# Half-wise loads of the first block, sink value rows by GpSimd transfers, joint sink scores and one more crossbar transpose in an attention and channel-mix kernel

## The chip, the cores and the metric

The kernel runs on one core of a Trainium2 chip. The metric is the time of one execution on the device in microseconds. Of the kernel before, three runs were timed; of one execution there is a profile with the start and end of every instruction.

## The reference

Sliding-window attention with four sink positions, and on its result an RWKV channel mix. Batch 4, 8 heads of 64, 768 positions, d_model 512, d_ff 1024.

```python
scores = scale * np.matmul(q, k.transpose(0, 1, 3, 2))
is_sink = pos[None, :] < int(n_sink)             # n_sink = 4
in_window = (rel >= 0) & (rel < int(window))     # window = 128
scores = np.where(is_sink | in_window, scores, -1e9)
a = softmax(scores); attn = np.matmul(a, v)
x = attn.transpose(0, 2, 1, 3).reshape(B, S, H * D)
x_prev = x shifted by one position
xk = mu_k * x + (1 - mu_k) * x_prev
xr = mu_r * x + (1 - mu_r) * x_prev
k = np.maximum(xk @ w_k, 0.0)
out = sigmoid(xr @ w_r) * ((k * k) @ w_v)
```

## The kernel before

The work is cut into 12 units: each of the 4 batches has three blocks of 256 positions (T is 0, 1, 2). A unit goes through four stages, one function each.

`load` issues the transfers of q, k and v on SP's queue. A unit's q and k come in two transfers each, one for each half of the partitions, and v in two for its two groups of 128 positions. `load_weight` issues the five 1 MB transfers of w_k (two halves, wka and wkb), w_r and w_v.

`prepare` casts q, k and v to bf16 (tiles kb, qb, vb; line L543 or L536), turns q and k so that the head dimension lies on the partitions, and copies them from PSUM to kt and qt (L589). The turning is done by PE transposes (L576), and for the units in KD and QD by the crossbar, a transposing transfer on SP's queue (L562). For T = 0 it also prepares the sinks. ksink holds the four sink keys of all heads (GpSimd, L670). vsink holds the four sink value rows of each head, each in the rows of that head: a matmul with the constant matrix spread copies the first four rows of vb to the partitions where they belong (L676), and VectorE multiplies them by hmask, which keeps one head in each row (L680).

`attend` computes a unit's scores (L721), exponentials on ScalarE (L775), masks on VectorE (L789) and products with v (L808), then 1/sum (L822) and x (L825). In blocks 1 and 2 of a batch the sinks lie outside the window, so scores with ksink (L696), their exponentials es (L703) and products with vsink (L763) are added. In block 0 the sinks lie inside the window or before it, and no such group is needed.

`mix` turns x into xt, by PE transposes (L849) and copies from PSUM (L858), or by the crossbar (L869) for the units in XD, which are 9, 10 and 11. It then forms the difference td (L877), xk and xr (L888). `ffn` has the products with w_k (L939), the relu (L949 on ScalarE, L953 on VectorE), its square kk (L967, L963), the products with w_r (L979) with the sigmoid (L985), and those with w_v (L997), whose result is multiplied (L1006) and stored (L1013). The last unit's last products are in `last_product` (L909, L919, L924).

The order of everything is fixed by three tables of numbers that were worked out outside the kernel. The functions only register operations in the list P.op; ORDER gives the order in which they are emitted (a negative number is a fill matmul on the tile warm, L1018, that computes nothing), CHOICE says which engine takes an operation that several could take, and SLOTS says which buffer each tile takes. Each engine runs its own instructions in that order and waits for the others by semaphores.

PSUM has two tiles of two banks for scores (sc) and four single banks (bank) for everything else, so a product's bank must be evacuated before another can be written to it. Loads of q, k and v have three buffers each, weights in fp32 three.

`fill`, `fill_later` and the `make_` functions set constants at the start. VectorE sets ones, spread, hmask, ksink, vsink and others, GpSimd makes ident, masks, spread and hmask. The casts of the weights follow the loads: w_k in four quarters, of which a unit's first products need the first.

Of the kernel before, what the change touches and what calls it, by code (L numbers as in the profile page):

```python
# [8 lines left out]
FP32 = mybir.dt.float32  # L9
# [9 lines left out]
    92: "ACT", 93: "ACT", 94: "ACT", 95: "ACT", 97: "ACT", 100: "ACT", 102: "DVE", 105: "DVE",  # L19
    110: "DVE", 111: "DVE", 114: "ACT", 115: "DVE", 139: "POOL", 142: "POOL", 145: "POOL", 148:  # L20
    "DVE", 150: "DVE", 151: "ACT", 152: "ACT", 154: "DVE", 161: "DVE", 191: "DVE", 193: "DVE",
    194: "DVE", 197: "DVE", 199: "DVE", 200: "DVE", 203: "DVE", 204: "DVE", 213: "DVE", 230:
    "ACT", 234: "ACT", 273: "DVE", 276: "DVE", 279: "DVE", 282: "DVE", 285: "ACT", 286: "ACT",
    298: "DVE", 306: "DVE", 315: "ACT", 354: "DVE", 364: "ACT", 365: "DVE", 367: "DVE", 383:
    "ACT", 387: "ACT", 436: "DVE", 439: "DVE", 444: "DVE", 445: "DVE", 467: "ACT", 475: "ACT",
    514: "DVE", 516: "DVE", 521: "DVE", 524: "ACT", 525: "ACT", 546: "ACT", 550: "ACT", 554:
    "ACT", 558: "ACT", 595: "DVE", 598: "DVE", 603: "ACT", 604: "ACT", 606: "DVE", 634: "ACT",
    681: "DVE", 682: "DVE", 691: "DVE", 700: "ACT", 704: "ACT", 708: "ACT", 755: "DVE", 759:
    "DVE", 760: "ACT", 772: "DVE", 781: "ACT", 785: "ACT", 789: "ACT", 834: "DVE", 836: "DVE",
    837: "DVE", 853: "ACT", 856: "DVE", 857: "ACT", 860: "DVE", 861: "ACT", 904: "DVE", 906:  # L30
    "DVE", 910: "DVE", 912: "DVE", 913: "DVE", 929: "ACT", 933: "ACT", 940: "DVE", 941: "ACT",
    994: "DVE", 995: "ACT", 999: "ACT", 1003: "ACT", 1007: "ACT", 1022: "DVE", 1026: "DVE",
    1034: "DVE", 1035: "ACT",
# [5 lines left out]
XD = (9,10,11)  # L39
# [7 lines left out]
JOINT = ()  # L47
# [5 lines left out]
BY_ACT = ()  # L53

# [131 lines left out]
def kernel(  # L186
# [14 lines left out]
    nc = tc.nc  # L201
# [198 lines left out]
    def fill():  # L400
        for t, value in ((ones, 1.0), (spread, 0.0), (hmask, 1.0)):
            nc.vector.memset(t, value)
        if VS:
            nc.vector.memset(pick, 0.0)
# [670 lines left out]
```

## Time and profile before

| what | value |
|---|---|
| median of 3 runs | 165.98 us (165.54 to 166.24) |
| span of the profiled execution, first to last instruction | 164.3 us |
| mean granted clock of TensorE | 0.999 |
| bytes moved | 34.60 MB, mean 211 GB/s |

The span is that of one execution under the profiler; the time of a run is taken around the whole execution and holds a little more than from the first to the last instruction, here 1.7 us. In the rows of the profile an engine with q behind its name (SPq) is its queue of issues, PEld is the weight load of PE. A row of a timeline gives the start, the time until its end, the engine, the line, the operation, the tile that is written and those that are read, and in brackets the idle time ahead of it and who ended it.

### The profile page before, as it was taken

The page shows a single profiled execution, that of the slowest core. Times are in us where ns is not written, and L with a number is a line of the kernel's source. Part 1 is how long each engine was busy: PE and PEld are TensorE (multiplying, and loading weights), DVE is VectorE, ACT ScalarE, POOL GpSimd, SP SyncE. Part 2 cuts the span into 40 slices and gives each one's busy share as a digit, 9 for nine tenths or more (in the row PEclk, how much of TensorE's full clock was granted, in tenths as well). Part 3 has the DMA queues.
Part 4 walks back from the last instruction along what each step waited for, and adds up shares of the span by engine and source line. Part 5 has one row for each costly group of instructions (what it writes and reads, how often), then busy time and mean ns, then how long its engine had stood idle before and what let it go on. Part 6 is the DMA issues. An engine that isn't in the chain of part 4 may idle for free.

```text
span 164.3 us, 4195 instructions
## 1 busy us (share of the span) xinstructions
PE 158.4 (96%) x1603; PEld 102.6 (62%) x1603; DVE 145.4 (89%) x381; ACT 131.2 (80%) x218; POOL 13.5 (8%) x38
## 2 busy tenths in 40 slices
PE   6999889999999999999999999999999999999992
PEld 2455568866467587577566775856575765664851
DVE  5259999999999999989999999999999999789752
ACT  3277999999999999999999999997668759163240
POOL 6409300010000000060000000000000000000000
PEclk9999999999999999999999999999999999999999
DMA  4999999999969896999999887986996955077743
GB/s 120 247 305 311 348 335 355 301 354 210 228 154 270 135 240 148 234 198 167 224 216 157 188 156 163 235 146 150 199 123 136 362 149 200 0 90 297 262 185 128
DMA packets 79042, 34.60 MB, mean 211 GB/s; under 512 B 67112, under 2 KB 73520, under 8 KB 79024
## 3 DMA queue, kind: packets, MB, share of 16 engines
q1 hardware_dynamic: 79008, 34.35, 86.3%
q8 instruction: 12, 0.20, 0.6%
q14 instruction: 6, 0.05, 0.1%
q10 hardware_dynamic: 16, 0.00, 0.0%
HBM read 24.12 MB, written 6.29 MB: 185 GB/s over the span
## 4 chain that ended last, share of the span: by engine, by line
PE 79%; ACT 8%; SPq 4%; DMA 3%; issue 2%; DVE 1%; POOL 1%; DVEq 0%; ACTq 0%; POOLq 0%
PE bank L997 23%; PE bank L939 23%; PE bank L979 12%; PE bank L808 6%; PE sc L721 6%; SPq L337 3%; DMA qs<-in_q_dram 3%; PE bank L576 2%; ACT e L775 2%; PE bank L849 2%; ACT rl L949 1%; PE bank L763 1%; ACT qt L589 1%; PE bank L909 1%; PE bank L1018 1%
## 5 line engine op out<-in xcount | busy, mean ns | idle before, releaser
L775 ACT ACTIVATE e<-sc 128x1024 bf16<-128x1024 f32 (+1 forms) x48 | 46.1, 994 | 1.8 <-PE sc L721 1.7
L939 PE MATMUL bank<-xk,wk_sb 128*128 128x256 bf16 x384 | 47.1, 273 | 0.0
L997 PE MATMUL bank<-wv_h,kk 128*128 128x512 bf16 x184 | 43.1, 379 | 0.1
L939 PEld LDWEIGHTS <-wk_sb 128*128 128x128 bf16 x384 | 36.4, 98 | 7.4 <-issue 0.4
L949 ACT ACTIVATE rl<-bank 128x512 bf16<-128x512 f32 x40 | 24.2, 625 | 8.6 <-PE bank L939 7.1
L997 PEld LDWEIGHTS <-kk 128*128 128x128 bf16 x184 | 17.1, 98 | 17.8 <-issue 0.4
L789 DVE TENSOR_TENSOR e<-e,mask 128x1024 bf16<-128x1024 bf16 (+1 forms) x40 | 25.4, 642 | 0.7 <-ACT e L775 0.5
L979 PE MATMUL bank<-wr_sb,xr 128*128 128x512 bf16 x96 | 23.7, 379 | 0.0
L888 DVE SCALAR_TENSOR_TENSOR xk<-td,mu_all,xt 128x256 bf16<-128x256 bf16 x48 | 22.4, 483 | 0.3
L888 DVE SCALAR_TENSOR_TENSOR xr<-td,mu_all,xt 128x256 bf16<-128x256 bf16 x48 | 22.1, 475 | 0.2
L967 ACT ACTIVATE kk<-rl 128x512 bf16<-128x512 bf16 x29 | 18.3, 664 | 4.2 <-DVE rl L953 4.0
L985 ACT ACTIVATE th<-bank 128x512 f32<-128x512 f32 x24 | 15.1, 646 | 5.7 <-PE bank L979 5.7
L825 DVE TENSOR_TENSOR x<-bank,rec 128x256 bf16<-128x256 f32 x48 | 19.2, 416 | 0.4
L808 PE MATMUL bank<-vb,e 128*128 128x65 bf16 x352 | 16.6, 194 | 0.0
L1006 DVE SCALAR_TENSOR_TENSOR w<-th,bank 128x512 f32<-128x512 f32 x19 | 13.0, 682 | 3.6 <-issue 1.8
L808 PEld LDWEIGHTS <-e 128*128 128x128 bf16 x352 | 13.6, 97 | 3.5
L979 PEld LDWEIGHTS <-xr 128*128 128x128 bf16 x96 | 8.8, 98 | 8.6 <-issue 0.2
L721 PE MATMUL sc<-qt,kt 64*128 64x128 bf16 (+1 forms) x256 | 13.9, 238 | 0.0
L721 PEld LDWEIGHTS <-kt 64*128 64x128 bf16 x256 | 8.9, 94 | 5.7 <-issue 3.1
L1018 PE MATMUL bank<-warm 128*128 128x512 bf16 x30 | 10.6, 484 | 1.1 <-DVE warm L1038 1.1
L877 DVE TENSOR_TENSOR td<-xt 128x512 bf16<-128x512 bf16 x24 | 10.3, 428 | 0.7 <-ACT xt L858 0.5
L589 ACT COPY qt<-bank 128x512 bf16<-128x512 bf16 x15 | 9.4, 643 | 1.0 <-PE bank L576 1.0
(74 smaller groups left out, 161.7 us busy)
## 6 DMA issues: line engine op xcount, KB each, us to landing
ks<-in_k_dram SPq DMA_DIRECT2D x24, 256.0 KB, 4.7
qs<-in_q_dram SPq DMA_DIRECT2D x24, 256.0 KB, 4.4
vs<-in_v_dram SPq DMA_DIRECT2D x24, 256.0 KB, 4.4
out_dram<-w SPq DMA_DIRECT2D x19, 256.0 KB, 2.7
w<-in_moe_w_k_dram SPq DMA_DIRECT2D x2, 1024.0 KB, 10.4
w<-in_moe_w_v_dram SPq DMA_DIRECT2D x2, 1024.0 KB, 9.3
w<-in_moe_w_r_dram SPq DMA_DIRECT2D x1, 1024.0 KB, 9.7
out_dram<-ob SPq DMA_DIRECT2D x4, 256.0 KB, 2.6
```

Of the source, the lines that this page charges most:

```text
L721: nc.tensor.matmul(out=sc[:, a, o0:o1], lhsT=lhs[rows], rhs=rhs[rows], start=u not in BIAS, stop=True, skip_group_check=u in BIAS)
L775: nc.scalar.activation(out=buf[ek][:, :, lo:], in_=buf[sck][:, :, lo:], func=AF.Exp, scale=scale)
L789: nc.vector.tensor_tensor(out=at, in0=at, in1=m, op=ALU.mult)
L808: nc.tensor.matmul(out=o[:, g, a, :], lhsT=e[:, a, e0:e0 + 128], rhs=rhs, start=(T == 0 and i == 0), stop=(i == len(blocks) - 1), skip_gro ...
L825: P.op("DVE", dve(256), lambda ok=ok, rk=rk, c=c: nc.vector.tensor_tensor(out=buf["x", u][:, :, 128 * c:128 * c + 128].rearrange("p g (a d ...
L888: nc.vector.scalar_tensor_tensor(out=buf[key][:, c, :], in0=buf[tk][:, i, :], scalar=mu[w][:, c:c + 1], in1=xt[:, c, t0 - 1:t0 + 255], op0 ...
L939: nc.tensor.matmul(out=ps[:, i, :], lhsT=wk_sb[:, c, 128 * f:128 * f + 128], rhs=xk[:, c, :], start=(c == 0), stop=(c == NC - 1), skip_gro ...
L949: nc.scalar.activation(out=buf[rk], in_=buf[psk].rearrange("p (i t) -> p i t", i=2), func=AF.Relu)
L967: nc.scalar.activation(out=buf["kk", u][:, 2 * f2:2 * f2 + 2, :], in_=buf[rk], func=AF.Square)
L979: nc.tensor.matmul(out=buf[psk], lhsT=buf["xr", u][:, c, 128 * g:128 * g + 128], rhs=wr_sb[:, c, :], start=(c == 0), stop=(c == NC - 1))
L985: P.op("ACT", act(512), lambda psk=psk, tk=tk: nc.scalar.activation(out=buf[tk], in_=buf[psk], func=AF.Tanh, scale=0.5), rank + 4 + g, tak ...
L997: nc.tensor.matmul(out=buf[psk], rhs=wv_h[:, f, :], lhsT=buf["kk", u][:, f, 128 * g:128 * g + 128], start=(f == 0), stop=(f == NF - 1))
```

## The change

The change has these parts:

- **Half-wise loads.** For units in BY_HALF (only unit 0) the q and k transfers are cut once more, by heads: eight transfers instead of four, first half of the heads of q, of k, then the second halves. `prepare` already works on halves of the heads.
- **Sink value rows.** A new fp32 tile vstage of 128 x 4 x 64 receives the four sink rows of v of all batches by four transfers of GpSimd, straight to the partitions where they belong. The product with hmask reads it there. The matmul with spread, spread itself and the bank that it needed go. The rows of a head move (from 4a to 16a within 32), so ksink and hmask change with them.
- **Joint sink scores.** JOINT becomes (0, 1, 2, 3): for each batch the scores with ksink and their exponentials are computed for blocks 1 and 2 together, in one bank and one activation of 512 columns.
- **Crossbar for unit 8.** XD becomes (8, 9, 10, 11).
- **Short memsets.** 20 one-column memsets of a tile spare on VectorE at the end of `fill_later`, 24 on GpSimd behind the mask. They compute nothing.
- **Tables.** CHOICE, ORDER and SLOTS are new throughout. ORDER has 26 fill matmuls instead of 30. In all, VectorE has 20 instructions more, which are the short memsets, and else 2 less; ScalarE has 1 less; GpSimd no longer takes the three casts of k and q that it had.

```diff
-XD = (9,10,11)
+XD = (8, 9, 10, 11)
-JOINT = ()
+JOINT = (0, 1, 2, 3)
+BY_HALF = (0,)
...
 ORDER = (
-    80, 81, 78, 82, 87, 83, 84, 77, -1, -2, -3, -4, -1, -2, 90, 0, 1, 79, 102, 108, -2, -3, -4,
+    80, 82, 84, 85, 83, 78, 2, 0, 77, 79, 108, 81, 92, -1, -2, -3, -4, -1, -2, -3, -4, 109, 93,
...
+            if u in BY_HALF:
+                rows = src[b, :, 256 * T:256 * T + 256, :].rearrange(
+                    "(w l) (p j) d -> w p l (j d)", w=2, j=4)
+
+                def by_half(key=key, rows=rows, half=0):
+                    for w in range(2):
+                        nc.sync.dma_start(
+                            out=buf[key][w::2, 4 * half:4 * half + 4, :, :].rearrange(
+                                "p (l x) j d -> p l (x j d)", x=2),
+                            in_=rows[w][:, 2 * half:2 * half + 2])
...
-    spread = tile1([128, 128], BF16, "spread")
+    vstage = tile1([128, B, D], FP32, "vstage")
+    spare = tile1([128, 48], FP32, "spare")
+
+    def short(engine, lo, hi):
+        for i in range(lo, hi):
+            engine.memset(spare[:, i:i + 1], 0.0)
...
-        for t in ksink + vsink:
+        for t in ksink + vsink + [vstage]:
             nc.vector.memset(t, 0.0)
...
+        short(nc.vector, 24, 44)
...
         window_mask(mask.rearrange("p k q -> p (k q)"), ones, 0.0)
+        short(nc.gpsimd, 0, 24)
...
-            keep(m, -4 * a, [[-32, NP], [0, D + 1]], 1, m)
-            keep(m, 3 + 4 * a, [[32, NP], [0, D + 1]], -1, m)
+            keep(m, -16 * a, [[-32, NP], [0, D + 1]], 1, m)
+            keep(m, 3 + 16 * a, [[32, NP], [0, D + 1]], -1, m)
...
+    for i in range(NS):
+        P.op("POOL", 1000.0, lambda i=i: nc.gpsimd.dma_start(
+            out=vstage[i::16], in_=v[:, :, i, :].rearrange("b h d -> h b d")), -50,
+            service=60.0, descs=32, reads=["stage0"], writes=[("vstage", i)])
...
-                nc.gpsimd.tensor_copy(out=kz[rows, :, 4 * a:4 * a + NS],
+                nc.gpsimd.tensor_copy(out=kz[rows, :, 16 * a:16 * a + NS],
...
-        P.op("PE", 220.0, lambda: nc.tensor.matmul(
-            out=buf[psk].rearrange("p (h d) -> p h d", h=H), lhsT=spread,
-            rhs=buf["vb", u][:, 0, :, 0:D], start=True, stop=True), rank + 4, lag=PE_LAG,
...
-            in0=buf[psk].rearrange("p (h d) -> p h d", h=H)), rank + 4, hold=[psk],
+                in0=vstage[:, b, :].unsqueeze(1).to_broadcast([128, H, D]))
```

Three places show how the tables move instructions. The first is the start of SP's queue, on which all loads are issued: first the kernel before, then the changed one (ks, qs and vs are the fp32 tiles of k, q and v; x2 stands for two issues alike).

```order
L337 DMA ks_67<-in_k_dram 64x4x256 x2
L337 DMA qs_70<-in_q_dram 64x4x256 x2
L307 DMA vs_73<-in_v_dram 128x8x64 x2
L337 DMA ks_68<-in_k_dram 64x4x256
L337 DMA qs_71<-in_q_dram 64x4x256 x2
```

```order
L353 DMA qs_70<-in_q_dram 64x2x256 x2
L353 DMA ks_67<-in_k_dram 64x2x256 x2
L353 DMA qs_70<-in_q_dram 64x2x256 x2
L353 DMA ks_67<-in_k_dram 64x2x256 x2
L320 DMA vs_73<-in_v_dram 128x8x64 x2
L368 DMA qs_71<-in_q_dram 64x4x256 x2
```

The four whole loads of unit 0 became eight half ones, with q ahead of k, and v of unit 0 stands behind eight issues instead of four.

The second is the same queue where the weights are loaded, before and then changed (w_76 and w_77 are buffers of the weights; ks_67 is unit 3's k here, vs_75 unit 2's v).

```order
L354 DMA w_76<-in_moe_w_k_dram 128x4x512
L354 DMA w_77<-in_moe_w_k_dram 128x4x512
L307 DMA vs_75<-in_v_dram 128x8x64
L337 DMA ks_67<-in_k_dram 64x4x256 x2
L354 DMA w_78<-in_moe_w_r_dram 128x4x512
L307 DMA vs_75<-in_v_dram 128x8x64
L337 DMA qs_70<-in_q_dram 64x4x256 x2
L354 DMA w_76<-in_moe_w_v_dram 128x4x512
```

```order
L385 DMA w_76<-in_moe_w_k_dram 128x4x512
L368 DMA ks_67<-in_k_dram 64x4x256 x2
L320 DMA vs_75<-in_v_dram 128x8x64 x2
L385 DMA w_77<-in_moe_w_k_dram 128x4x512
L368 DMA qs_70<-in_q_dram 64x4x256 x2
L385 DMA w_78<-in_moe_w_r_dram 128x4x512
L385 DMA w_76<-in_moe_w_v_dram 128x4x512
```

Four loads of 256 KB moved ahead of the second half of w_k.

The third is ScalarE's queue up to its cast of the first quarter of w_k (wk_sb), before and then changed (e are the exponentials, es those of the sinks, kt, qt and xt copies from PSUM).

```order
L775 ACTIVATE e_97<-sc_62 128x1024
L775 ACTIVATE e_93<-sc_61 128x1024
L589 COPY kt_86<-bank_63 128x2x256
L703 ACTIVATE es_98<-bank_66 128x256
L589 COPY qt_91<-bank_64 128x2x256
L646 CAST vb_136<-vs_74 128x8x64
L775 ACTIVATE e_94<-sc_61 128x1024
L589 COPY qt_91<-bank_65 128x2x256
L775 ACTIVATE e_95<-sc_62 128x1024
L703 ACTIVATE es_99<-bank_65 128x256
L501 ACTIVATE wk_sb<-w_76 128x4x256
```

```order
L626 COPY kt_86<-bank_65 128x2x256
L683 CAST vb_136<-vs_74 128x8x64
L741 ACTIVATE es_98<-bank_66 128x512
L813 ACTIVATE e_93<-sc_62 128x1024
L813 ACTIVATE e_95<-sc_61 128x1024
L580 CAST kb_81<-ks_69 128x2x4x64
L896 COPY xt_155<-bank_63 128x2x256
L626 COPY kt_87<-bank_64 128x2x256
L626 COPY kt_87<-bank_63 128x2x256
L813 ACTIVATE e_96<-sc_62 128x1024
L538 ACTIVATE wk_sb<-w_76 128x4x256
```

The cast of w_k moved behind unit 2's k (kt_87) and a fifth wide exponential; the two es of 256 columns became one of 512. From the first exponential to this cast ScalarE had 18 instructions and now has 23. At the other end of the program, unit 11's x, which ends the chain of dependent work, goes to the crossbar behind unit 11's last value products; between those and the first product that needs it PE had 32 key products and 40 products of 512 columns, and now has 16 and 40.

More of the change, by code (lines that the diff above doesn't have):

```diff
@@ L18 @@
 CHOICE = {
[L19 to L30, printed above, removed]
@@ L446, in make_bias1 @@
         window_mask(early.bitcast(BF16)[:, 384:640], warm[:, 0:128], LOW)
-    def make_spread():
-        for a in range(2):
-            nc.gpsimd.tensor_copy(
-                out=spread[0:NS, :].rearrange("p (c w) -> p c w", w=32)[:, :, 4 * a:4 * a + NS],
-                in_=ident[0:NS, 0:NS].unsqueeze(1).to_broadcast([NS, NP, NS]))
     def make_hmask():
```

57 lines of the change are left out of this document (46 added, 11 removed), and 154 rows, old and new, of tables (ORDER, SLOTS).

## The prediction

> **What bounds the kernel now.** I read the page first: busy shares, slices, chain.
>
> ```profile
> PE 158.4 (96%) x1603; PEld 102.6 (62%) x1603; DVE 145.4 (89%) x381; ACT 131.2 (80%) x218; POOL 13.5 (8%) x38
> ...
> PE   6999889999999999999999999999999999999992
> ...
> ACT  3277999999999999999999999997668759163240
> ...
> PEclk9999999999999999999999999999999999999999
> ...
> PE 79%; ACT 8%; SPq 4%; DMA 3%; issue 2%; DVE 1%; POOL 1%; DVEq 0%; ACTq 0%; POOLq 0%
> ```
>
> PE is busy nearly always and carries 79% of the chain, at a clock that was never cut. But ACT's row is at 9 as well for two thirds of the span, so I ask next where PE is the limit and where it waits. The table by stretches gives, after each stretch and its length, the busy time of PE, PEld, DVE, ACT and POOL, the clock, the DMA share and GB/s.
>
> ```profile
> 12.00:18.00 6.00, 5.29 (x68) 3.17 (x66) 5.71 (x17) 4.67 (x8) 5.23 (x13) 1.00 1.10 304
> 18.00:24.00 6.00, 5.44 (x85) 3.55 (x85) 5.93 (x19) 6.00 (x11) 0.00 (x0) 1.00 1.08 360
> 24.00:44.00 20.00, 20.00 (x212) 14.00 (x212) 19.79 (x52) 20.00 (x33) 0.74 (x2) 1.00 1.03 299
> ...
> 104.00:124.00 20.00, 20.00 (x207) 13.18 (x205) 19.65 (x54) 16.16 (x28) 0.00 (x0) 1.00 0.99 166
> ```
>
> From 24 us on PE has no gap to speak of. Before that it has gaps, and DVE and ACT set the pace (5.93 and 6.00 of 6.00 in 18 to 24). So there are two questions: when does the gapless part start, and how much PE work is left from there. The timeline of PE (start, us, engine, line, what) shows the start, the first products with wk (L939), and what matmuls cost when they follow each other.
>
> ```profile
> 16.77 0.38 PE L676 MATMUL bank<-vb,spread 128*128 128x512 bf16 x1
> 16.99 0.39 PE L576 MATMUL bank<-ident,kb 128*128 128x128 bf16 x4
> ...
> 23.54 0.59 PE L1018 MATMUL bank<-warm 128*128 128x512 bf16 x2
> 23.98 1.05 PE L939 MATMUL bank<-xk,wk_sb 128*128 128x256 bf16 x8
> 24.87 0.39 PE L849 MATMUL bank<-ident,x 128*128 128x128 bf16 x4
> 25.09 0.39 PE L576 MATMUL bank<-ident,kb 128*128 128x128 bf16 x4
> ...
> 128.80 0.93 PE L939 MATMUL bank<-xk,wk_sb 128*128 128x256 bf16 x7
> 129.66 0.29 PE L696 MATMUL bank<-qt,ksink 128*32 128x256 bf16 x4
> 129.88 0.61 PE L721 MATMUL sc<-qt,kt 64*128 64x256 bf16 x12
> ```
>
> A matmul costs the distance to the next start, not its own 0.2 to 0.4 us: 0.22 for 512 columns (16.77 to 16.99, and two in 23.54 to 23.98), 0.111 for 256 (eight in 0.89), 0.055 for 128 (four in 0.22). A group of four sink scores takes 0.22, and entering it 0.08 more (seven products of 0.111 are 0.78, the distance is 0.86).
>
> **The change, part by part: PE after the start.** Removed behind the first wk product are three of the four spread products (the first lies ahead of it): 3 x 0.22 = 0.66. Unit 8's x goes by crossbar, which drops eight transposes: 8 x 0.055 = 0.44. Joint sink scores turn two groups of four into one of eight; four of them run side by side, so the second four add 0.11 where a group of its own costs 0.22 + 0.08: 0.19 less for each batch, 0.57 for the three behind the start. Sum: **1.67 us less**. The fill matmuls (30 to 26), and the same savings of batch 0, lie ahead of the start in time that PE waits through, and are worth nothing.
>
> **The start.** It is set by ACT, whose queue must get through the exponentials of units 0 and 1 before its cast of the first wk quarter (L501). Rows of ACT and of the first DVE cast:
>
> ```profile
> 7.61 0.43 DVE L543 CAST qb<-qs 128x512 bf16<-128x512 f32 x1 [2.31 <-DMA qs<-in_q_dram]
> ...
> 9.91 1.51 ACT L775 ACTIVATE e<-sc 128x768 bf16<-128x768 f32 x2
> ...
> 12.80 1.51 ACT L775 ACTIVATE e<-sc 128x768 bf16<-128x768 f32 x2 [0.55 <-PE sc L721]
> 14.20 0.59 ACT L589 COPY qt<-bank 128x512 bf16<-128x512 bf16 x1
> ...
> 16.68 1.94 ACT L775 ACTIVATE e<-sc 128x1024 bf16<-128x1024 f32 x2 [0.31 <-PE sc L721]
> 18.51 0.59 ACT L589 COPY kt<-bank 128x512 bf16<-128x512 bf16 x1
> 18.98 0.41 ACT L703 ACTIVATE es<-bank 128x256 bf16<-128x256 f32 x1
> 19.25 0.62 ACT L589 COPY qt<-bank 128x512 bf16<-128x512 bf16 x1
> 19.72 0.66 ACT L646 CAST vb<-vs 128x512 bf16<-128x512 f32 x1
> 20.29 1.02 ACT L775 ACTIVATE e<-sc 128x1024 bf16<-128x1024 f32 x1
> ...
> 22.85 1.08 ACT L501 ACTIVATE wk_sb<-w 128x1024 bf16<-128x1024 f32 x1
> ```
>
> Distances from start to start: 0.70 for a narrow exponential (12.80 to 14.20, two), 0.915 for a wide one (16.68 to 18.51), 0.47 for a copy, 0.57 for a cast, 0.27 for es. Before, ACT has 18 instructions from the first exponential to the wk cast: 4 narrow, 4 wide, 6 copies, 2 casts, 2 es, together 10.96, in 12.94 us; so some 2 us are waits. The new order puts 23 there: 4 narrow, 5 wide, 9 copies, 4 casts and one es of 512 (I take a copy's 0.47): 2.80 + 4.58 + 4.23 + 2.28 + 0.47 = **14.4 us**, 3.4 more. Three casts that GpSimd did are part of it.
>
> Against that stands an earlier first exponential. The landing of q ends the wait at 7.61, and 2.3 us later (cast, transpose, copy, scores) comes the exponential at 9.91. The DMA issues and the landing medians:
>
> ```profile
> 0.81 1.41 SPq L337 DMA_DIRECT2D ks<-in_k_dram  x2
> 2.27 1.27 SPq L337 DMA_DIRECT2D qs<-in_q_dram  x2
> ...
> out_dram<-w SPq DMA_DIRECT2D x19, 256.0 KB, 2.7
> ...
> w<-in_moe_w_k_dram SPq DMA_DIRECT2D x2, 1024.0 KB, 10.4
> ...
> out_dram<-w SPq DMA_DIRECT2D x2, 128.0 KB, 1.7
> ```
>
> Four issues took 2.9 us however large the transfers are, so the four first halves are issued by about 3.5, the last at about 2.9. Before, the last of four whole ones was issued there too, and landed 4.7 us later. A half-size store landed 1.0 us sooner than a whole one (1.7 against 2.7), and half the bytes lie ahead: I bound the last first half by 5.1 and 6.6 and take 5.7. The first exponential is then at 8.0 (7.4 to 8.9), some 1.9 us sooner.
>
> The Trainium skill, "DMA: Bandwidth & Descriptors", "Rules for kernel authors", speaks against splitting: two transfers to disjoint partition halves serialize, and one large transfer is better. The rows above agree that a transfer of half the size takes well over half the time (1.7 of 2.7), but they also show it landing sooner; this kernel split by partitions before already. If by that rule nothing at all were gained, it would be the last rival below.
>
> Waits of ACT in the new stretch: 1.5 us (0.5 if all that it does is fed, 3 if unit 1's k, which lands about as late as before, holds it). From the start of the wk cast to the first product 1.1 (22.85 to 23.98). Start: 8.0 + 14.4 + 1.5 + 1.1 = **25.0**, against 23.98: 1.0 later. DVE must also do some 40 instructions from unit 0's v to its own wk cast, and v stands behind four more issues; this ends no earlier, so I give the start no less than 23.4.
>
> **Parts that I cost at nothing.** The memsets on spare run on DVE while it waits for q and k, and on GpSimd, which has nothing to do from 18 to 24 us (0.00 of 6.00). GpSimd's four loads of sink rows: no such transfer is in the trace; vsink is first needed at about 17 us and they are issued by about 9, so even the 10.4 of the largest transfer would cost 2 us at most, the 2.7 of a store nothing; I take 0. Unit 8's two crossbar transposes add two issues to SP's queue, ahead of later keys' transposes: 0 to 1.0 us, I take 0. At the end, unit 11's x:
>
> ```profile
> 142.79 3.65 SPq L869 DMA_TRANSPOSE xt<-x  x2
> ...
> xt<-x SPq DMA_TRANSPOSE x6, 3.5
> ...
> 152.41 3.49 PE bank L939 x32
> ```
>
> Before, PE has other work for 9.6 us between these transposes and the first product that needs them. Behind unit 11's last value products stood 32 key products and 40 of 512 columns, 32 x 0.111 + 40 x 0.22 = 12.4; now 16 and 40 stand there, 10.6, and the 9.6 shrink to 7.8. If landing (3.5, the second issued 1.2 later) and DVE's differences and mixing take the whole of 9 us, PE waits 1.2. I count 0: nothing shows that the 9.6 were used up.
>
> **Sum.** Span 164.3 + 1.0 - 1.67 = 163.6. The median of the runs, 165.98, lies 1.7 above the profiled span. **165.3 us**.
>
> **Rivals.** (a) *The earlier scores are carried through.* With the exponential at 7.4 and waits of 0.5 the start is at 23.4: 164.3 - 0.6 - 1.67 = 162.0, so 163.7; if also the gapless part loses less than now, down to 162.6. For it: nothing but DMA holds the first scores. Against: DVE's 5.93 of 6.00.
>
> (b) *Weights late, slower.* The second half of wk was issued as the second of these two and landed 10.4 later:
>
> ```profile
> L354 SPq DMA_DIRECT2D w<-in_moe_w_k_dram x2: 676/1310/1943, 13.6 to 14.3; - x2
> ```
>
> That is 24.7. Now unit 3's k and unit 2's v, four loads of 256 KB, stand ahead of it. At 360 and 299 GB/s their 1.05 MB take 2.9 and 3.5 us, the additional issues up to 2.4: it lands at 27.6 to 30.6. Its cast on DVE or ACT takes 1.1, behind perhaps one exponential of 0.9: ready at 28.7 to 32.6. PE needs it after 32 key products (3.55), 12 transposes (0.66) and two half groups of scores with their value products (about 1.2): 25.0 + 5.4 = 30.4. At the late end PE waits 2.2 us: 167.5. It is slower by the bound below once the cast ends after 31.9. In all three later weights the same lateness is then already paid. For it: PE has no reserve behind 24 us, ACT is at 20.00 of 20.00. Against: the middle of the range, 30.6, costs next to nothing.
>
> (c) *The halves do not land sooner.* First exponential at 9.9 as before, start at 26.9: 164.3 + 2.9 - 1.67 = 165.5, so 167.2. Against it stand the two stores.
>
> **How the numbers follow.** A difference of 0.5% (0.83 us: 165.15 and 166.81) is about what a measurement of this kernel can tell from no change. Forecast 0.42, rival (a) 0.27, (b) 0.22, (c) 0.09. The forecast lies just inside the bound, and its own spread (164.5 to 166.6) is cut by it: 0.16 of its 0.42 count as faster. Of (b) and (c) 0.06 stay within the bound. Faster 0.43, same 0.32, slower 0.25. The range leaves out about one in ten at each end: 162.7 to 167.5.
>
> **What would show it.** Right: the first exponential near 8.0; the first wk product at 25 with a gapless PE behind it; a PE whose remaining work is 1.7 us shorter; sink score groups of eight with 0.33 to the next. Wrong: a wait of PE on the wk, wr or wv casts after 29 us (b); a first exponential after 9 (c); a start before 24 (a); a wait of PE for xk in the last 20 us, or of DVE for the sink rows at 17. If the stalls that PE has within 24 to 160 us shrink or grow, which I hold equal, the sum is wrong at that place.

## The result, and the profile after

| what | before | after |
|---|---|---|
| median of 5 runs | 166.07 us (165.54 to 166.40) | 168.12 us (167.12 to 168.60) |
| span of the profiled execution | 164.3 us | 166.9 us |
| ratio after to before | | 1.0105 [1.0072, 1.0138] |

The change makes the kernel about 1% slower. The profiled execution took 168.60 us and is the longest of the five; the spans of the others are 165.4 to 166.4 us, and the time around the span is 1.7 us in all of them. So what the rows below lose is more than a usual execution loses; the unaltered kernel was profiled once more as e18, with a span of 165.3 us. The page of the changed kernel, with the same rows as before: busy shares, slices of PE, ACT and the clock, and the chain that ended last by engine.

```profile
PE 158.9 (95%) x1587; PEld 101.8 (61%) x1587; DVE 143.7 (86%) x399; ACT 132.2 (79%) x217; POOL 12.0 (7%) x61
...
PE   7998979999999899999899999999999999999991
...
ACT  3467999999999998997999999969678949532350
PEclk9999999999999999999999999999999999999999
...
PE 14%; DMA 3%; DVE 2%; issue 0%; SPq 0%; DVEq 0%
```

PE's row now has two slices at 8 in the stretch that was all 9 before. The chain was 79% PE before, and now it can be followed back only to a transfer. In order of time it begins (start, us, what):

```profile
133.69 4.05 DMA xt<-x
...
137.83 0.77 DVE td L915 x2
138.59 0.79 DVE xk L926 x2
...
140.83 0.27 PE bank L977
```

A crossbar transpose (unit 10's x), the differences that wait for it, xk, and the product that waits for xk: a transfer, not PE, was last here. PE was idle for only 0.13 us ahead of that product, so this row shows the kind of the wait and not what was lost. The table by stretches (PE, PEld, DVE, ACT, POOL, clock, DMA share, GB/s) tells how much PE lost, where before had 19.89 us or more in each of these stretches:

```profile
44.00:64.00 20.00, 19.20 (x210) 12.45 (x208) 18.32 (x48) 18.60 (x33) 0.00 (x0) 1.00 1.08 222
64.00:84.00 20.00, 19.56 (x207) 12.75 (x204) 19.15 (x54) 18.66 (x33) 0.60 (x2) 1.00 1.13 208
...
104.00:124.00 20.00, 19.68 (x194) 11.71 (x192) 19.23 (x51) 16.33 (x28) 0.00 (x0) 1.00 1.07 157
```

The three have 1.56 us without PE work, at a full clock. The start shows in ScalarE's timeline, as in the prediction:

```profile
9.01 1.51 ACT L813 ACTIVATE e<-sc 128x768 bf16<-128x768 f32 x2 [1.45 <-PE sc L759]
...
11.66 1.51 ACT L813 ACTIVATE e<-sc 128x768 bf16<-128x768 f32 x2 [0.60 <-PE sc L759]
...
14.78 0.62 ACT L580 CAST kb<-ks 128x512 bf16<-128x512 f32 x1 [1.11 <-DMA ks<-in_k_dram]
...
17.19 1.94 ACT L813 ACTIVATE e<-sc 128x1024 bf16<-128x1024 f32 x2 [0.22 <-PE sc L759]
...
22.77 0.67 ACT L580 CAST kb<-ks 128x512 bf16<-128x512 f32 x1
23.46 0.58 ACT L896 COPY xt<-bank 128x512 bf16<-128x512 bf16 x1
23.94 1.16 ACT L626 COPY kt<-bank 128x512 bf16<-128x512 bf16 x2
25.09 1.02 ACT L813 ACTIVATE e<-sc 128x1024 bf16<-128x1024 f32 x1
26.01 1.05 ACT L538 ACTIVATE wk_sb<-w 128x1024 bf16<-128x1024 f32 x1
```

and VectorE's cast of w_k:

```profile
25.66 0.69 DVE L544 CAST wk_sb<-w 128x1024 bf16<-128x1024 f32 x1
```

The first exponential is 0.9 us sooner than before (9.01 against 9.91), but ScalarE's queue waits for unit 1's k until 14.78, and the first product with w_k comes at 26.41 instead of 23.98, when VectorE's cast has ended. The landing medians of loads and crossbar transposes, after:

```profile
qs<-in_q_dram SPq DMA_DIRECT2D x4, 128.0 KB, 2.6
ks<-in_k_dram SPq DMA_DIRECT2D x4, 128.0 KB, 2.7
kt<-kb SPq DMA_TRANSPOSE x16, 3.8
...
qt<-qb SPq DMA_TRANSPOSE x8, 4.1
...
vstage<-in_v_dram POOLq DMA_DIRECT2D x4, 8.0 KB, 2.9
```

and before:

```profile
kt<-kb SPq DMA_TRANSPOSE x16, 3.6
...
qt<-qb SPq DMA_TRANSPOSE x8, 2.4
```

Four key times carry the comparison from here on (first exponential, first product with w_k, start of the last matmul, span):

| | exponential | w_k product | last matmul | span |
|---|---|---|---|---|
| before | 9.91 | 23.98 | 160.83 | 164.25 |
| after | 9.01 | 26.41 | 163.28 | 166.90 |

From the first w_k product to the last matmul it is 136.85 us before and 136.87 after. So 2.43 us were lost at the start, none were won behind it, and 0.2 us went in the last stores.

### The profile page after: what moved, and what is told of

Read it like the earlier page. It is cut to its first block, busy times and chain, and to the rows that moved or that the text cites. A ratio compares the mean times of both kernels' runs of the same rounds, so it can differ in the third digit from the quotient of the medians.

```text
span 166.9 us, 4218 instructions
## 1 busy us (share of the span) xinstructions
PE 158.9 (95%) x1587; PEld 101.8 (61%) x1587; DVE 143.7 (86%) x399; ACT 132.2 (79%) x217; POOL 12.0 (7%) x61
## 5 line engine op out<-in xcount | busy, mean ns | idle before, releaser
L813 ACT ACTIVATE e<-sc 128x1024 bf16<-128x1024 f32 (+1 forms) x48 | 45.0, 959 | 4.3 <-PE sc L759 4.3
L977 PE MATMUL bank<-xk,wk_sb 128*128 128x256 bf16 x384 | 48.0, 273 | 0.3
L1035 PE MATMUL bank<-wv_h,kk 128*128 128x512 bf16 x184 | 44.0, 379 | 0.1
L987 ACT ACTIVATE rl<-bank 128x512 bf16<-128x512 f32 x44 | 25.7, 606 | 7.4 <-PE bank L977 6.3
L827 DVE TENSOR_TENSOR e<-e,mask 128x1024 bf16<-128x1024 bf16 (+1 forms) x40 | 25.2, 644 | 0.1
L926 DVE SCALAR_TENSOR_TENSOR xk<-td,mu_all,xt 128x256 bf16<-128x256 bf16 x48 | 21.7, 479 | 0.1
L1023 ACT ACTIVATE th<-bank 128x512 f32<-128x512 f32 x24 | 14.2, 601 | 8.7 <-PE bank L1017 8.5
L1005 ACT ACTIVATE kk<-rl 128x512 bf16<-128x512 bf16 x24 | 14.8, 632 | 2.8 <-DVE rl L991 2.7
L1044 DVE SCALAR_TENSOR_TENSOR w<-th,bank 128x512 f32<-128x512 f32 x18 | 12.1, 684 | 2.0 <-PE bank L1035 1.3
L683 ACT CAST vb<-vs 128x512 bf16<-128x512 f32 x17 | 10.5, 634 | 1.2 <-DMA vs<-in_v_dram 1.2
L1001 DVE TENSOR_TENSOR kk<-rl 128x512 bf16<-128x512 bf16 x24 | 9.8, 415 | 1.8 <-ACT rl L987 1.8
```

Source lines behind the costliest of these rows:

```text
L813: nc.scalar.activation(out=buf[ek][:, :, lo:], in_=buf[sck][:, :, lo:], func=AF.Exp, scale=scale)
L827: nc.vector.tensor_tensor(out=at, in0=at, in1=m, op=ALU.mult)
L926: nc.vector.scalar_tensor_tensor(out=buf[key][:, c, :], in0=buf[tk][:, i, :], scalar=mu[w][:, c:c + 1], in1=xt[:, c, t0 - 1:t0 + 255], op0 ...
L977: nc.tensor.matmul(out=ps[:, i, :], lhsT=wk_sb[:, c, 128 * f:128 * f + 128], rhs=xk[:, c, :], start=(c == 0), stop=(c == NC - 1), skip_gro ...
L987: nc.scalar.activation(out=buf[rk], in_=buf[psk].rearrange("p (i t) -> p i t", i=2), func=AF.Relu)
L1005: nc.scalar.activation(out=buf["kk", u][:, 2 * f2:2 * f2 + 2, :], in_=buf[rk], func=AF.Square)
```

## The experiments

Two questions: what sets the start, and where the saved PE work went. Three theories are named below. **L**: the start is set by the landing of unit 1's k and the queue behind it, not by the first exponential. **H**: behind the start VectorE's queue paces the changed order. **D**: behind the start transfers come late. "Start" is the first product with w_k, "behind" the time from it to the last matmul. All ratios are to the kernel before, run on the same chip. Of each run one execution was profiled; times within a run are from that one.

**What sets the start.** The first four edits are of the changed kernel. In e1 the casts of the first two quarters of w_k come sooner, one on VectorE and one on ScalarE, and four fills go; ScalarE's part of the edit:

```diff
+L538 ACTIVATE wk_sb<-w_76 128x4x256
 L813 ACTIVATE e_96<-sc_62 128x1024
-L538 ACTIVATE wk_sb<-w_76 128x4x256
```

> The changed kernel with the casts of the first two quarters of w_k moved forward (VectorE's ahead of the difference td of unit 1, ScalarE's ahead of unit 2's first exponential) and the four fill matmuls ahead of the first w_k product taken out. The weight has landed at 23.8 us. Theory P (PE's own work from the first product sets the end): the first product starts near 25.4 instead of 26.4 and the whole run is about 1.0 us faster than the changed kernel. Theory H (ScalarE and VectorE set the pace in the middle, PE only waits elsewhere): the first product is as early, but the run changes by less than 0.3 us, since the casts only change places with exponentials.

170.28 us, 1.0243 [1.0207, 1.0280]. The first exponential was at 7.82, the start at 26.12, 0.3 us sooner than after instead of the expected 1.0, and "behind" became longer, 139.08 us: the sigmoids (L1023) are 0.2 us later than after's at first, up to 0.4 sooner in between and 1.9 later at the end. Neither expectation held; moving the casts ahead gave nothing.

In e2 four fills are added between 5 and 8 us, where PE has gaps, to see whether its slow first products come from these.

```diff
+four fill matmuls among unit 0's first transposes and scores (ORDER)
```

> The changed kernel with four more fill matmuls between 4.8 and 8 us, where its PE has gaps. If PE's slow pace there (0.32 us for 384 columns where 0.16 is seen later) comes from these gaps, the four bias products take 0.65 instead of 1.3 us, the first exponential starts at about 8.2 instead of 9.0, and by theory P the end comes 0.5 to 0.8 us earlier if ScalarE's queue passes it on. If the slow pace has nothing to do with the gaps, the bias products stay at 0.32 each and the first exponential comes at 9.0 to 9.4.

168.66 us, 1.0158 [1.0119, 1.0196]. The exponential came sooner than in after, 8.16, and the start was at 26.81, not sooner but 0.4 later. An earlier exponential is worth nothing here. That the fills made it earlier is not shown: it was at 8.28 in e18, without them.

e3 loads unit 0 whole, in the changed order.

```diff
-BY_HALF = (0,)
+BY_HALF = ()
```

> The changed kernel with unit 0's q and k loaded whole (four issues of 256 KB, q first), all else as it is. If half loads bring the start forward, the first exponential comes later than 9.0, at about 9.5 to 10, and the first w_k product later than 26.4 by as much; the run is 0.5 to 1.0 us slower than the changed kernel. If the four additional issues cost more than the halves bring, all later loads land some 2 us of issue time earlier (v of unit 0 near 9.7 instead of 10.7), the first product comes at 25 to 26 and the run is faster by 0.5 or more.

170.81 us, 1.0285 [1.0240, 1.0330]; exponential 11.52, start 29.11, both later than expected. In the changed order, with q ahead of k, the half loads are worth 2.7 us at the start.

e7 issues the two first halves of unit 0's k from ScalarE, so that SP has two issues less ahead of unit 1.

```diff
-                        nc.sync.dma_start(
+                        queue = nc.scalar if key[0] == "k" and half == 0 else nc.sync
+                        queue.dma_start(
```

> The changed kernel with the two transfers of the first half of unit 0's k issued by ScalarE's queue instead of SP's, so that all later loads are issued 1.3 us sooner; ScalarE issues them ahead of its table load. Theory L (the start is set by the loads of units 1 and 2, which the four additional issues push back): unit 1's k lands near 13.4 to 13.8 instead of 14.7, the first w_k product comes at 25.2 to 25.8 instead of 26.4, and the run is 0.6 to 1.2 us faster than the changed kernel. Theory A (ScalarE's longer queue from the first exponential on sets it): no change of the first product beyond 0.3 us.

168.67 us (167.56 to 169.19), 1.0171 [1.0138, 1.0203]. ScalarE's timeline of e7:

```profile
7.80 1.51 ACT L814 ACTIVATE e<-sc 128x768 bf16<-128x768 f32 x2 [0.60 <-PE sc L760]
...
14.28 0.62 ACT L581 CAST kb<-ks 128x512 bf16<-128x512 f32 x1 [1.83 <-DMA ks<-in_k_dram]
...
25.51 1.05 ACT L539 ACTIVATE wk_sb<-w 128x1024 bf16<-128x1024 f32 x1
```

and of e6 (below), which leaves the start alone:

```profile
7.68 1.51 ACT L813 ACTIVATE e<-sc 128x768 bf16<-128x768 f32 x2 [0.60 <-PE sc L759]
...
15.12 0.62 ACT L580 CAST kb<-ks 128x512 bf16<-128x512 f32 x1 [1.83 <-DMA ks<-in_k_dram]
...
26.34 1.05 ACT L538 ACTIVATE wk_sb<-w 128x1024 bf16<-128x1024 f32 x1
```

The exponentials differ by 0.12, the casts of unit 1's k by 0.84, and the casts of w_k by 0.83 as well. Over eight executions of the changed order (after, e2, e6, e7, e9, e13, e17, e18) this cast starts at 14.28 to 15.19, the exponential at 7.68 to 9.01, and the distance from the cast to the start is 11.62 us in every one. (In e3 and e15, whose loads come otherwise, it was 12.80 and 12.96.) So L holds; it rests on this distance and not on e7's shift, since the cast was at 14.46 in e18 without the edit. For the total e7 gave nothing: its start is 25.90, 0.5 sooner (25.2 to 25.8 was expected), and its median is no better than after's, so what is lost behind the start varies by more than that.

e8 puts the half loads alone into the old order.

```diff
+BY_HALF = (0,)
```

> The kernel before with the half-wise loads alone (k's first half, q's, then the second halves; the cast of k's second half moved behind the copy of the first), its order otherwise unchanged. By theory L the first exponential comes 1 to 1.5 us sooner (8.4 to 8.9 instead of 9.9), unit 1's loads 1 us or more later, and the first w_k product is not earlier than 24.0; the run is 0.3 to 1.5 us slower than the kernel before. If the earlier scores are carried through, the first product comes near 23 and the run is about 1 us faster.

167.94 us, 1.0103 [1.0071, 1.0136]. Exponential 10.17, not sooner than before's 9.91, start 25.09, 1.1 us late, and 1.08 to 1.11 late at each of the 24 sigmoids up to the end. In the old order, where k goes ahead of q, the halves cost about as much as the whole change, and the old order passes a late start on one for one. (About 0.4 of the 1.7 us lies outside the span: 2.3 us around it against 1.9.) L holds in the old order too: unit 1's k lands at 13.36 in before and at 14.47 in e8, and the start follows 10.62 us later in both.

**Is the saved PE work worth anything?** These four have the sink rows by transfers in the old order, with spread and its products gone (0.66 us of PE work behind the start), and differ in who issues the transfers and who multiplies.

```diff
-    spread = tile1([128, 128], BF16, "spread")
+    vstage = tile1([128, B, D], FP32, "vstage")
+        e4, e16: P.op("POOL", ... nc.gpsimd.dma_start(out=vstage[i::16], ...
+        e11, e12: P.op("ACT", ... nc.scalar.dma_start(out=vstage[i::16], ...
 vsink multiplied by GpSimd for all batches (e4), for batches 1 to 3 (e12), by VectorE for all (e11, e16)
```

> The kernel before, its order unchanged, with the sink value rows by GpSimd's four transfers: the four spread products and the bank they need are gone, nothing else. Theory P: three of the four lie behind the first w_k product, 0.66 us less than the kernel before. Theory H: PE waits for others by as much, within 0.2 us of the kernel before. If the transfers come late, VectorE waits for them near 17 us and the run is slower.

> The kernel before, order unchanged, with the sink value rows loaded by four transfers that ScalarE issues at 3 to 5.5 us, where it waits for k, and the product with hmask on VectorE as before (in the run with GpSimd's transfers that product ran on GpSimd, 1.1 us, ahead of ksink). The four spread products go. If the late start of that run came from GpSimd, the first w_k product is back at 24.0 +- 0.2; by theory P 0.66 us of PE work less behind it, the run 0.4 to 0.7 us faster than the kernel before.

> As the run with ScalarE's transfers, but the product with hmask of batches 1 to 3 on GpSimd, which is idle then: 0.68 us less on VectorE three times. By theory P for the old order no further gain beyond 0.2 us; if VectorE holds PE there, up to 1 us faster than the run with all four on VectorE. A loss would be GpSimd's ksink copies coming late behind these products.

> The kernel before, order unchanged, with the sink value rows by GpSimd's four transfers and the product with hmask on VectorE, so that GpSimd's ksink copies are not held up. The run with ScalarE's transfers showed the PE work gone (0.57 of 0.66 us from the first w_k product on) but a start at 24.8. If the start comes back to 24.0 to 24.3 here, the run is 0.2 to 0.6 us faster than the kernel before, and beats both kernels; if the four small transfers cost the first loads as much whoever issues them, it is within 0.3 us of the kernel before or slower.

| | median | ratio | start | late at start | late at the last sigmoid |
|---|---|---|---|---|---|
| e4 | 167.61 | 1.0088 [1.0065, 1.0111] | 25.51 | 1.53 | 1.38 |
| e11 | 166.76 | 1.0033 [1.0014, 1.0053] | 24.84 | 0.86 | 0.28 |
| e12 | 167.95 | 1.0097 [1.0072, 1.0122] | 25.56 | 1.58 | 1.43 |
| e16 | 166.11 | 0.9995 [0.9974, 1.0015] | 24.77 | 0.79 | 0.21 |

e4 and e12 were confounded: GpSimd's multiplication stands ahead of the ksink copies, and in both the lateness first grows, to 1.93 and 1.98 at the fifth sigmoid, which it doesn't in e11 and e16. Those are the clean ones. In both, the time behind the start is 136.28 us against 136.85, and the lateness shrinks by these 0.57 us in three steps, of the 0.66 that I summed. So a saved PE product is worth its time where the order is held by PE.

All four start later than before, by 0.8 us even at best, and no version here beats the kernel before. In e16 the late start goes with unit 1's k again: it lands at 14.04 instead of 13.36, and the start follows after 10.73 us. Whether the sink transfers delay it is not shown: in e5, e10 and e14, which change nothing ahead of unit 3, this k lands at 13.54, 14.40 and 13.53, and the start follows after 10.6 to 10.7 us, at 25.06 in e10. So a start 0.8 us late in one profiled execution is within what the old order shows without an edit there.

**H: does VectorE pace the changed order?** e5 and e6 leave the masks out from unit 3 on and move squares (kk) from ScalarE to VectorE, 24 in the kernel before and 18 in the changed one; e10 and e9 leave out the masks alone, in the one and in the other.

```diff
+                if u >= 3:
+                    masked = lambda: None
 CHOICE (e5, e6 only): 24 and 18 entries of kk from "ACT" to "DVE"
```

> The kernel before with less work for VectorE and ScalarE from unit 3 on: the mask products of the exponentials are left out (36 of 40, about 0.6 us each on VectorE), and the 24 squares that ScalarE had there go to VectorE (0.64 us each off ScalarE, 0.42 more on VectorE). PE's work and order are the same. Theory P (PE is the bound): within 0.5 us of the kernel before. Theory H (the two engines set the pace): faster by more than 1 us.

171.85 us, 1.0334 [1.0273, 1.0395]. This one misfired: the squares piled up on VectorE, and PE waited for them.

```profile
PEld L997 <- DVE kk L963: 4.7, 2, 2.9
...
PE bank L997 <- DVE kk L963: 3.7, 2, 2.4
```

(Engine, line, waited for: us, times, longest.) It says that moving work between engines in a fixed order makes waits of its own, and nothing about H.

> The changed kernel with the same relief: mask products from unit 3 on left out, 18 squares from ScalarE to VectorE. Its PE has 1.67 us less work behind the first w_k product than the kernel before, but took as long for it. Theory P: no gain, it stays 2 us above the kernel before. Theory H: the 1.67 us come out, that is, from the first w_k product to the last matmul it takes 1.5 us less or more than that in the changed kernel (136.9), and less than the relieved kernel before by about as much.

169.92 us, 1.0234 [1.0179, 1.0289]. Up to 130 us it ran as much as 2.5 us ahead of after, then lost 1.8 of that within 10 us, where PE waited for a square once more (1.7 us at the longest), and nearly all the rest by the end. It doesn't decide H either.

> The changed kernel with the mask products of the exponentials left out from unit 3 on (36 of 40, 0.6 us each on VectorE), and nothing moved to another engine. Theory H (in the changed order VectorE and ScalarE, not PE, pace the middle): from the first w_k product to the last matmul it takes 1.5 to 3 us less than the 136.9 of the changed kernel, and the run is faster by as much. Theory P: within 0.5 us of the changed kernel.

> The kernel before with the same mask products left out, nothing moved. The kernel before is taken to be bound by PE from the first w_k product on (136.9 us to the last matmul, without gaps): its time stays within 0.7 us of the kernel before. If it gains 1.5 us or more here too, VectorE paced the middle in both kernels, and that is then no difference between them.

e9: 168.69 us (167.01 to 169.69), 1.0124 [1.0084, 1.0163]; e10: 166.19 us, 1.0000 [0.9978, 1.0022]. VectorE fell to 14 to 16 of 20 us in each stretch of e9 from 44 us on, and the changed kernel was not faster. H falls. What the two orders differ in shows in the waits. In before the only wait of PE, VectorE or ScalarE behind the start that a transfer ended is

```profile
PEld L721 <- DMA vs<-in_v_dram: 0.2, 1, 0.2
```

and in after there are, among others,

```profile
DVE td L915 <- DMA xt<-x: 2.7, 2, 1.7
...
ACT vb L683 <- DMA vs<-in_v_dram: 1.2, 1, 1.2
...
DVE vb L683 <- DMA vs<-in_v_dram: 1.0, 1, 1.0
...
PE sc L759 <- DMA qt<-qb: 0.3, 1, 0.3
```

With the smaller ones they come to 6.2 us in after and to 4.6 in e18. These are waits of all three engines together, not time that PE lost, so they raise the question of the transfers and do not answer it.

**D: are the transfers late?** e13 and e14 leave out the loads of v from unit 3 on, in the changed kernel and in the one before; 18 loads of 256 KB, 4.7 of 34.9 MB.

```diff
-... lambda queue=queue, key=key, g=g, s0=s0: queue.dma_start(
+... lambda queue=queue, key=key, g=g, s0=s0, u=u: u < 3 and queue.dma_start(
```

> The changed kernel with the v loads of units 3 to 11 left out (18 transfers of 256 KB; their casts read what the buffers hold from earlier units). Theory D (behind the start the changed order is held by transfers that land too late: its engines wait for k, q, v, kt, qt and xt after 30 us, those of the kernel before do not): with 4.7 MB and 18 issues less the other transfers land sooner, the waits go, and from the first w_k product to the last matmul it takes 1.2 to 2 us less than the 136.9 of the changed kernel; the spread of its runs shrinks. Theory H2 (ScalarE's queue paces the middle): within 0.5 us of the changed kernel.

> The kernel before with the same v loads left out. It waits for no transfer behind its start, so by theory D its time stays within 0.5 us of the kernel before. If it gains as much as the changed kernel does, late transfers are no difference between the two.

e13: 166.35 us (165.84 to 166.79), 0.9996 [0.9976, 1.0016]; e14: 166.17 us, 0.9991 [0.9970, 1.0012]. The stretches of e13:

```profile
64.00:84.00 20.00, 20.00 (x201) 12.74 (x199) 19.41 (x53) 19.76 (x36) 0.00 (x0) 1.00 0.67 141
84.00:104.00 20.00, 20.00 (x229) 13.78 (x229) 19.36 (x51) 19.72 (x33) 0.39 (x2) 1.00 0.88 160
104.00:124.00 20.00, 20.00 (x227) 12.92 (x224) 19.10 (x52) 16.05 (x27) 0.00 (x0) 1.00 0.44 93
```

and its crossbar transposes:

```profile
kt<-kb SPq DMA_TRANSPOSE x16, 2.9
...
qt<-qb SPq DMA_TRANSPOSE x8, 2.7
```

With less to transfer the transposes land in 2.9 and 2.7 us instead of 3.8 and 4.1, PE has no gap left from 64 to 124 us, and behind the start it takes 134.15 us instead of 136.87. The whole stretch from the first w_k product to the last matmul, in before, after and e13:

```profile
23.98:160.83 136.85, 136.70 (x1387) 90.96 (x1387) 128.23 (x327) 114.90 (x193) 3.62 (x6) 1.00 0.87 200
26.41:163.28 136.87, 134.97 (x1355) 89.13 (x1356) 123.78 (x317) 113.45 (x189) 2.17 (x6) 1.00 0.94 207
26.37:160.52 134.15, 133.81 (x1355) 88.90 (x1356) 123.08 (x317) 113.18 (x189) 1.60 (x6) 1.00 0.68 173
```

PE was idle in it for 0.15, 1.90 and 0.34 us; the rest of the 2.7 us that e13 gains is a shorter busy time for the same products. The runs also lie closer together (0.95 us from lowest to highest instead of 1.5). The old order gains nothing from the same relief (behind the start 136.66 against 136.85). D holds: it is the changed order that has no slack for its transfers. ScalarE has the same work in e13 as in after, so H2 of the expectation falls. The loads of v left out stop landing late themselves, make room for the others and shorten SP's queue by 18 issues; the run does not part these three.

e15 has GpSimd issue those 18 loads, to ask whether SP's queue of issues makes them late.

```diff
-                    queue, by = ... else (nc.sync, "SP")
+                    queue, by = (nc.gpsimd, "POOL") if u >= 3 else (nc.sync, "SP")
```

> The changed kernel with the v loads of units 3 to 11 issued by GpSimd, which has little else to do, instead of SP: the same bytes, but SP's queue, in which a load stands behind each transpose that waits for its cast, gets 18 issues shorter. If the queue of issues is what makes transfers late, the run is 0.5 to 1.5 us faster than the changed kernel; if it is the bytes that the DMA engines can move, there is no gain, and a loss if GpSimd's transfers take longer to start or push k and q back.

177.97 us, 1.0701 [1.0626, 1.0776]. Far slower, and transfers now make up a quarter of the chain (by engine, e15):

```profile
PE 46%; DMA 23%; ACT 13%; SPq 7%; DVE 6%; issue 3%; ACTq 0%; DVEq 0%
```

It does not answer the question cleanly, since some loads then stand on GpSimd behind copies of ksink that wait 10 us for their keys. Whether SP's queue or the bytes make the transfers late stays open.

**Two last questions.** e17 leaves out the short memsets, e18 is the changed kernel unaltered, to see how firm its 1.0105 is.

```diff
-        short(nc.vector, 24, 44)
-        short(nc.gpsimd, 0, 24)
```

> The changed kernel without its 44 one-column memsets on the tile spare (20 on VectorE, 24 on GpSimd), nothing else. My term for them was 0: the start follows the landing of unit 1's k, which they do not touch, so cast of that k to first w_k product 11.6 us again, first product at 25.9 to 26.8, and a median of 167.5 to 168.7. Rival: the memsets hold VectorE's first casts or GpSimd's four sink transfers, and without them the start is earlier by their sum on the engine: the memsets end at about 5 us, so at most 1 us, and the median would be 167.1 to 167.4.

> The changed kernel itself, with no edit, beside the kernel before. It was 1.0105 [1.0072, 1.0138] of the kernel before; variants of it that should have been neutral gave 1.0158, 1.0171 and, without the short memsets, 1.0209. If the transfers make the changed order's time wander between chips and runs by more than the interval, this gives something from 1.013 to 1.021 and the short memsets count for nothing. If 1.0105 holds (1.007 to 1.013), leaving out the memsets cost about 1%.

e17: 170.1 us (168.85 to 171.63), 1.0209 [1.0171, 1.0248]. e18: 167.9 us (166.96 to 169.20), 1.0111 [1.0075, 1.0146]. The result is firm, and leaving out the memsets costs about 1.6 us (the difference of the ratios, 0.0098, of 166.2), which no term of mine foresaw and neither theory of the expectation. That the memsets themselves help is not shown: e2 and e7, small edits at the start as well, came out at 1.0158 and 1.0171. The distance from unit 1's k to the start is 11.62 us as ever. About 0.7 us lie outside the span (2.3 to 2.5 us around it in every run of e17, 1.7 in e18), the rest within it. Why is open. The time around the span differs in other runs too (1.7 us in after, 1.9 in the kernel before beside these runs, 2.1 in e16). e18's profiled execution shows how far the waits vary in one kernel: start 26.08, behind 135.55, 1.3 us less than in the execution shown above.

## Why the prediction was wrong

Forecast 165.3 us with a range up to 167.5; measured 168.12. In the profiled execution the summed span of 163.6 became 166.9. The 3.3 us are made of four pieces:

- **Stalls held equal: +2.7 us.** This is the step that failed most. The prediction said "If the stalls that PE has within 24 to 160 us shrink or grow, which I hold equal, the sum is wrong at that place", and had no price for it. They grew: behind the start after takes 136.87 us, where the work that PE has left gives 136.85 - 1.67 - 0.99 = 134.2 (the 0.99 is the third piece). With the loads of v out it takes 134.15; the old order gains 0.2 from the same. e9 took VectorE off the list, e13 and e14 name the transfers. A hint stood in the prediction's own rows, a DMA share of 1.03 and 0.99.
- **The start: +1.4 us.** The sum 8.0 + 14.4 + 1.5 + 1.1 = 25.0 let ScalarE's queue run on from the first exponential. But the queue stops for unit 1's k, which the prediction named as a bound only ("3 if unit 1's k, which lands about as late as before, holds it"), and this k was not as early as before. It landed at 14.7 against 13.4, behind four more issues of about 0.65 us each. From its cast there are 11.62 us to the first product, in which ScalarE hardly waits. The right sum is 14.8 + 11.6 = 26.4; with a landing at 13.4 it would be an estimated 25.1. So the 25.0 would have come out but for this landing, by luck, since the path that it was summed along does not set the start. Term by term it was 9.0 for the exponential, 1.9 of waits (0.60 + 1.11 + 0.22), 15.1 of queue up to the cast at 26.01, where 14.4 was summed, and 0.4 from there, since the quarter that was needed first was cast by VectorE (25.66 to 26.35) and not by ScalarE. Had the exponential come sooner, the wait for k would have been longer, as in e6 and e7.
- **Work moved ahead of the start: -1.0 us.** Besides the 1.67 us, the new order puts 8 more transposes (8 x 0.055 = 0.44) and 12 more score products, 4 of 256 columns and 8 of 128, ahead of the first w_k product, while PE waits there anyway. Such a group took 0.55 us to the next (rows below; the first row is 4 of 256 and 8 of 128). Together PE has 2.66 us less behind the start; PE's busy time there is 136.51 in e14 and 133.81 in e13, a difference of 2.70. I counted only the removed work, not what a later start lets through.
- **The last stores: +0.2 us.**

163.6 + 2.7 + 1.4 - 1.0 + 0.2 = 166.9. These are the pieces of the longest of the five executions. In e18's, with a span of 165.3, the same sum is 163.6 + 1.4 + 1.1 - 1.0 + 0.2: there the start cost nearly as much as the stalls. PE's timeline of after, for the score products:

```profile
24.59 0.62 PE L759 MATMUL sc<-qt,kt 64*128 64x256 bf16 x12
25.14 0.40 PE L887 MATMUL bank<-ident,x 128*128 128x128 bf16 x4
```

The other steps:

- **PE work per product** was right: 0.57 of the 0.66 came through in the old order, and a group of eight sink scores takes 0.33 us to the next product, as forecast.
- **Half loads.** The last first half landed at 5.58 us, where 5.7 was taken, and so rival (c) fell. (Its four issues take 2.7 us in the prediction's rows, 0.81 to 3.54, not 2.9; nothing hangs on it.) The Trainium skill, "DMA: Bandwidth & Descriptors", "Rules for kernel authors", says that two transfers to disjoint partition halves serialize and that one is better. The new cut is by heads, so this rule does not speak of it directly. Here what a cut is worth depends on the order: +2.7 us without the halves in the changed one (e3), +1.1 us with them in the old one (e8).
- **The first exponential**, 8.0 forecast, 9.01 measured in the profiled execution and 7.7 to 8.3 in the other seven. The forecast was right, and it did not matter. That it would set the start was wrong.
- **Rival (b)**, weights late: the second half of w_k landed at 31.4, later than the 27.6 to 30.6 given, but PE's weight load waited for wk_sb only 0.7 us in all (row below), 0.5 of it at the start and 0.2 at 32.2 us for this half. It named the right kind of cause, a late transfer, at the wrong place.
- **Sink rows** landed within 3.8 us and VectorE did not wait for them: right. **Unit 11's x**: VectorE waited 1.7 us for its transpose, but PE's other work covered it: right, at 0. **Memsets** at 0: not borne out, the kernel is slower without them (e17).

The wait of after that rival (b) is judged by (us, times, longest):

```profile
PEld L977 <- DVE wk_sb L544: 0.7, 2, 0.5
```

Not tried: unit 8's crossbar alone and the joint sink scores alone. Which of the moved transfers takes the slack stays open too.

## What to carry to other kernels

Before summing a saved product on a PE that is busy 96% of the time, ask of the new order when each transfer is issued and how long before its use: with DMA near a share of 1.0, a new order can lose in waits for transfers all that it saves in work, and leaving out some of the loads in a trial of both orders shows that. A start behind several loads was set here by the one that ended the last long wait in the queue, so walk the queue back from its end to that landing and count the issues ahead of it. To know which start counts, look for a distance that stays constant over executions (here 11.62 us) rather than for what comes first.

## What was not expected of the hardware

PE's first matmuls ran at two paces under a granted clock shown as 1.0. Four products of 384 columns, first in after:

```profile
6.73 1.49 PE L766 MATMUL sc<-ob,ident 128*128 128x384 bf16 x4
8.15 0.82 PE L759 MATMUL sc<-qt,kt 64*128 64x256 bf16 x8
```

and in e18, another execution of the same kernel:

```profile
6.89 0.81 PE L766 MATMUL sc<-ob,ident 128*128 128x384 bf16 x4
7.73 0.50 PE L759 MATMUL sc<-qt,kt 64*128 64x256 bf16 x8
```

1.42 us against 0.84 to the next group. The Trainium skill, "TensorE: Matmul & The Clock Gate", "Part 1: The HAM clock gate (the "warmup" mystery)", says that the gate's window is free-running, so that the number of slow matmuls at the start differs from run to run; the two traces agree in that the slow phase differs between executions of one kernel, though the clock's row shows full speed in both. No trace here shows the window.

Without 44 one-column memsets at the start the kernel was about 1.6 us slower (e17 against e18), 0.7 of it outside the span. 18 loads issued by GpSimd made it 6% slower than the changed kernel (177.97 against 168.12 us), with a landing median of 6.9 us against 4.1 from SP; the Trainium skill, "SBUF — State Buffer", "Summary: rules for kernel authors", advises issuing a transfer that is to be hidden under VectorE work from ScalarE's or SP's queue instead. No run here shows whether its reason applies: in e15 GpSimd's loads and copies also waited in its own queue, up to 13 us at a time.
